# A state read followed by causal expert attention on one core: a new issue order, ScalarE's table asked for first, and 13 zero multiplications at the start left out

## The chip, the core and the metric

The kernel runs on one core of a Trainium2 chip. A core has TensorE (PE; its weight loads are listed as PEld), VectorE (DVE), ScalarE (ACT), GpSimd (POOL) and SyncE (SP), which issues every transfer here. The engines run side by side, each through its own list of instructions in order, and wait for each other by semaphores. The metric is the device time of one execution in microseconds (us).

## What is computed

There are two stages. For each of 8 batches and 8 heads, 512 rows of `x` and 32 rows of `state` (64 wide) attend to each other; the results, 544 rows of 512 columns in a batch, feed a causal attention with 4 experts, of which a gate takes the best two for each row:

```python
scores = scale * x @ state.T          # softmax over 32, then @ state -> xread
scores2 = scale * state @ x.T         # softmax over 512, then @ x    -> sread
x = concat([xread, sread])            # per batch: 544 rows, 512 columns
logits = x @ w_gate                   # two best of 4 experts, softmax of the two
for e in range(4):
    q, k, v = x @ wq[e], x @ wk[e], x @ wv[e]
    a = softmax(where(causal, -1e9, scale * q @ k.T))
    out += weight_of(e) * (a @ v @ wo[e])
```

Values that need more than fp16 are kept as two fp16 parts (high and low), and a product is the sum of three matmuls. The first batch is done in fp32 instead.

## The kernel before, in words

The kernel is a list of 2034 numbered steps. A step is one instruction of ACT, DVE, POOL or SP, or a group of matmuls; some steps have two or three ways, on different engines. Steps are first collected (`st.do`, `st.mm`, `st.dma`), batch by batch: `front` (loads `xn` and `sn`, transposes, the row softmax in `eb`, the attention `at` and the weights `gs` folded with the state, the gate, and `qm`, `kt`, `v`), `side` (the state's own rows), `main` (`probs`: scores, the exponential in `p`, its parts in `ph`, transposed by a transfer to `pt`; then `reads`: `pt` times `v`, scaled into `z`, split into `zh`, transposed by a transfer to `z`, multiplied by `wo_n`, and written out) and `tail` (the 32 last rows of two batches together).

Nothing in this text decides when a step runs. `run()` (line 346) goes through the table `ORDER` and issues the steps in that order. An entry such as `81.0.3` is step 81, way 0, and 3 zero multiplications ahead of it (line 360: 128x512 matmuls of the tile `zeros` into the PSUM bank that the step will write). The table `SLOTS` says which of several buffers each tile takes. Since each engine works through its list in order, the table decides what stands behind what on each engine, on SP's list of transfers too. Every step's instruction is recorded at line 362 (the call in `run()`), so rows of the profile are told apart by their tiles.

At the start, `zeros` is set by DVE (line 398). Step 0 is nine zero multiplications (`WARM=9`), which read no input. Steps 1 to 5 load the first batch's `sn` and `xn` (in four pieces of 256 KB, two for each half of the rows) and steps 7 and on the weights `wk`, `wq`, `wv` into three buffers `p`, each in a piece of three experts (384 KB) and one of one expert (128 KB). In `first` (line 662) step 8 transposes `sn` on TensorE, which ACT turns into the block-diagonal `tqf`; steps 69, 71, 131 and 133 transpose four tiles of `xn` (eight fp32 multiplications by `ident` each); steps 73 and 135 are the scores (`bank<-tqf,xT`); 83, 86 and 89 multiply the weights by the state (`bank<-p,tqf`), and 81 and 143 transpose the softmax's result (`bank<-ident,eb`).

Of batch 3 (counted from 0), step 977 is the transfer that transposes the probabilities of its last row block into `pt` (16 tiles of 128x128), and step 998 is the group of matmuls that reads them.

Of the kernel before, what the change touches and what calls it, by code (L numbers as in the profile page):

```python
# [9 lines left out]
F32 = mybir.dt.float32  # L10
# [19 lines left out]
2.0 3.0 44.0 42.0 32.0 61.0 52.0 33.0 56.0 55.0 51.0 0.0.2 186.0 184.0 1.0 8.0.11 69.0 185.0 71.0 5.0 4.0 131.0 30.0 31.0 11.0 13.0 38.0 50.0 64.0  # L30
65.0 62.0 6.0 66.0 7.0 67.0 133.0 9.0 70.0 10.0 188.0 72.1 187.0 189.0 190.0 132.0 191.0 73.0 134.0 198.0 201.0 74.0 75.0 76.0 135.0 218.0 86.0 136.0
77.0 68.0 63.0 137.0 88.0 87.0 78.1 79.0 222.0 12.0 83.0 324.0 322.0 207.0 85.0 138.0 80.1 323.0 89.0 139.0 91.1 22.0 47.0 54.0 40.0 28.0 43.0 46.0
58.0 48.0 18.0 140.0 203.0 141.0 142.1 81.0.3 195.0 204.0 82.0 325.0 90.0 223.1 336.0 119.0 143.0 333.0 144.0 206.0 337.0 205.0 326.0 96.0 172.0
210.0 330.0 120.1 334.0 92.0 149.0 145.0 331.0 219.0 224.0 45.0 53.0 41.0 14.0 327.0 173.0 35.0 93.0 97.0 239.0 100.0 211.0 328.0 24.0 200.1 26.0
15.0 29.0 202.1 16.0 19.0 199.1 60.0 338.0 192.0 84.1 101.0 104.0 102.0 105.0 103.0 98.0 150.0 99.0 146.0 153.0 154.0 157.0 209.1 106.0 107.0 231.1
155.0 158.0 121.0 226.1 147.0 335.0 159.0 122.0 332.0 94.0 329.0 108.0 156.0 160.0 109.1 174.0 161.0 162.1 175.0 240.0 197.1 148.0 110.0 180.0 176.0
123.0 163.0 111.0 164.0 165.0 112.0 220.1 95.0 166.0 113.0 167.0 168.0 114.0 170.0 171.0 151.0 115.0 181.0 118.0 117.0 152.0 124.0 221.0 228.0 193.1
208.1 232.0 196.1 182.0 339.0 177.0 125.0 340.0 347.0 346.0 127.0 588.0 37.0 233.0 348.0 128.0 229.0 194.1 230.0 591.0 225.1 241.0 183.0 169.0 126.0
116.0 341.1 342.0 178.0 179.0 243.0 592.0 593.0 442.0 244.0 129.0 130.0 242.0 370.0 343.0 358.0 246.0 359.0 245.0 360.0 252.0 253.0 349.1 227.0 594.0
344.1 350.0 351.0 254.0 255.0 345.0 247.1 373.0 249.0 20.0 34.0 443.0 361.1 248.0 352.1 362.0 439.0 265.0 266.0 256.0 250.2 257.0 258.0 353.0 259.0  # L40
590.0 215.0 444.0 589.0 375.0 374.0 363.0 267.0 268.0 445.1 251.0 262.1 364.1 376.0 354.0 234.0 365.0 595.0 1069.0 212.0 377.0 263.0 355.0 235.0
# [12 lines left out]
498.0 17.0 25.0 651.0 659.0 474.0 483.1 817.0 716.0 564.0 653.0 661.0 662.0 471.0 301.0 654.0 821.0 837.0 663.0 836.0 668.0 825.0 669.0 565.0 1079.0
818.0 717.0 822.1 664.0 665.0 1082.0 823.0 501.0 655.0 923.0 666.0 1080.0 1083.0 1070.0 484.0 316.0 718.0 670.0 719.0 503.0 485.0 683.0 667.0 720.0
671.0 824.0 317.0 819.1 504.0 486.0 826.0 499.0 562.0 1085.0 820.0 1084.0 698.0 515.0 1283.0 502.1 693.0 1086.0 838.0 672.0 566.0 567.0 673.0 924.0
36.0 21.0 505.0 674.0 675.0 487.0 920.0 506.0 684.0 488.0 516.0 827.1 676.0 686.0 689.0 828.0 1076.0 677.0 678.0 679.0 681.0 682.0 694.0 829.0 507.0
839.1 840.0 489.0 921.0 695.0 690.0 319.0 702.0 696.0 830.1 831.0 685.0 841.0 699.0 687.0 691.0 692.0 1081.0 318.0 1087.0 925.0 700.1 508.0 832.0
842.1 680.0 568.0 320.0 1077.0 703.0 517.1 520.0 697.0 848.0 853.0 843.0 688.0 704.0 1078.0 917.1 521.0 849.0 856.0 851.0 1284.0 854.0 833.0 569.0
705.0 701.0 522.0 512.0 509.0 857.0 852.0 850.0 721.0 722.0 730.0 731.0 922.0 706.0 1282.0 724.0 723.0 1281.0 1285.0 855.0 733.0 732.0 734.0 844.0  # L60
518.0 513.0 1088.0 834.0 835.0 523.1 510.0 845.0 1092.0 1095.0 570.0 725.1 726.0 727.0 743.0 728.0 511.0 1548.0 572.0 736.0 735.0 846.0 1093.1 729.0
737.1 519.0 738.0 524.0 571.0 573.0 574.0 918.0 1089.0 740.1 1094.0 1194.0 575.0 576.0 577.0 744.0 758.0 759.0 926.0 745.0 741.0 746.0 1096.0 1108.0
919.0 1189.1 1547.0 847.0 59.0 896.0 739.0 525.0 760.0 761.0 1107.0 927.0 1109.0 1090.1 747.1 1091.0 578.0 579.0 749.0 893.0 862.0 866.0 753.0 1191.1
1195.0 1196.0 1192.1 1292.0 742.1 762.0 1110.0 748.0 1295.0 897.0 763.0 764.0 750.1 751.0 1193.0 898.0 1296.0 1297.0 858.0 928.0 894.0 1111.0 859.0
929.0 863.0 768.1 867.0 1286.0 754.0 1097.0 1188.1 771.0 870.0 871.0 895.0 930.0 765.0 772.0 878.0 1098.1 755.1 1293.0 874.0 1099.0 879.0 880.0
1112.0 875.0 580.0 756.0 868.0 860.0 1100.0 876.0 869.0 1101.1 1113.1 864.0 526.0 1289.0 877.0 881.0 861.0 581.1 1102.0 304.0 903.0 529.0 882.0 766.0
# [1123 lines left out]
```

## Time and profile before

| | us |
|---|---|
| median of 3 runs | 292.83 |
| lowest and highest | 290.92, 296.96 |
| the profiled execution | 294.01 |
| its span in the profile | 292.2 |

In the span PE is busy 274.2 us, DVE 246.0, ACT 212.5 and POOL 198.2. The profile lists for every engine its instructions with start and length, and for each idle stretch what released the engine at its end. Three views are used: sums by stretch of time, the chain of work that ended last, and instructions in order of time. A matmul row with a count merges neighbours of one kind; fp32 multiplications count twice.

### The profile page before, as it was taken

To read this page: it belongs to the slowest core of one execution; us is meant where nothing else is said; L and a number is where in the kernel's file an instruction comes from. 1 tells how busy PE (TensorE), PEld (TensorE's weight loads), DVE (VectorE), ACT (ScalarE), POOL (GpSimd) and SP (SyncE) were. 2 spreads that over 40 slices of the span, in tenths; PEclk is the share of its full clock that TensorE was granted. 3 is DMA by queue.
4 is the path that set the end of the run, shared out by engine and by line. 5 is a ranking of instruction groups with operands and counts; after the bars stand their busy time and mean duration, and the time that the engine had idled before them with its cause. 6 is when DMAs were issued, how large, how long until landed. Compare 5 with 4: busy or idle time off the path is not lost.

```text
span 292.2 us, 9588 instructions
## 1 busy us (share of the span) xinstructions
PE 274.2 (94%) x3587; PEld 184.1 (63%) x3587; DVE 246.0 (84%) x787; ACT 212.5 (73%) x685; POOL 198.2 (68%) x268
## 2 busy tenths in 40 slices
PE   8989996989999989999999959999999999999994
PEld 3857753557557644877657637776566757666862
DVE  1489999999999988998999997989999987886540
ACT  3668897789889888987988885744977566366632
POOL 7144895688978988699985729989587646556200
PEclk9999999899999999999999999999999999999999
DMA  7946599899999999999999899998938966899673
GB/s 197 193 136 127 104 249 176 219 168 155 236 228 157 222 161 272 198 192 242 217 208 165 199 182 238 206 200 160 160 64 146 184 133 84 207 194 188 143 248 122
DMA packets 154574, 53.19 MB, mean 182 GB/s; under 512 B 140576, under 2 KB 150048, under 8 KB 154528
## 3 DMA queue, kind: packets, MB, share of 16 engines
q1 hardware_dynamic: 154528, 52.59, 94.6%
q8 instruction: 28, 0.46, 0.7%
q14 instruction: 18, 0.15, 0.1%
HBM read 11.02 MB, written 8.91 MB: 68 GB/s over the span
## 4 chain that ended last, share of the span: by engine, by line
PE 59%; DVE 26%; DMA 7%; issue 4%; ACT 2%; POOL 2%; DVEq 0%; ACTq 0%
PE bank L362 57%; DMA pt<-ph 5%; DVE xh L362 4%; DVE bank L362 3%; DVE gs L362 2%; DVE qf L362 2%; DVE sbm L362 2%; DMA qm<-qh 2%; DVE eb L362 2%; PE bank L360 2%; DVE m L362 2%; DVE mb L362 1%; DVE z L362 1%; DVE et L362 1%; POOL qh L362 1%
## 5 line engine op out<-in xcount | busy, mean ns | idle before, releaser
L362 PE MATMUL bank<-gs,at 128*128 128x260 f16 (+3 forms) x368 | 51.4, 285 | 1.8 <-ACT e L362 1.0
L362 PE MATMUL bank<-kt,qm 128*128 128x128 f16 (+13 forms) x368 | 48.0, 313 | 2.2 <-DMA qm<-qh 1.1
L362 PE MATMUL bank<-v,pt 128*128 128x192 f16 x480 | 44.0, 247 | 6.0 <-DMA pt<-ph 3.4
L362 PE MATMUL bank<-wo_n,z 128*128 128x512 f16 (+1 forms) x198 | 46.1, 373 | 1.0 <-DMA z<-zh 0.6
L362 PEld LDWEIGHTS <-pt 128*128 128x128 f16 x480 | 40.5, 98 | 9.6 <-DMA pt<-ph 6.6
L362 POOL TENSOR_TENSOR ph<-p,ph 128x1024 f16<-128x1024 f32 (+3 forms) x25 | 36.0, 1443 | 7.3 <-ACT ph L362 2.9
L362 PEld LDWEIGHTS <-at 128*128 128x128 f16 x336 | 32.7, 99 | 11.3 <-issue 3.3
L362 ACT ACTIVATE p<-bank,mx 128x128 f32<-128x128 f32 (+3 forms) x64 | 33.2, 525 | 3.5 <-DVE mx L362 2.6
L362 DVE CUSTOM_DVE_ANT_0 bank<-bank,causal 128x128 f32<-128x128 f32 (+3 forms) x64 | 30.6, 504 | 4.3 <-PE bank L362 4.0
L362 PEld LDWEIGHTS <-qm 128*128 128x128 f16 (+1 forms) x336 | 20.1, 96 | 18.0 <-issue 5.9
L362 PEld LDWEIGHTS <-z 128*128 128x128 f16 x198 | 18.6, 98 | 19.3 <-DMA z<-zh 1.2
L362 ACT ACTIVATE o<-bank 128x512 f32<-128x512 f32 (+1 forms) x35 | 20.3, 587 | 9.8 <-PE bank L362 9.2
L362 PE MATMUL bank<-at,gs 128*128 128x512 f16 (+1 forms) x100 | 24.7, 382 | 0.7 <-ACT at L362 0.7
L362 DVE SCALAR_TENSOR_TENSOR xh<-xn,xh 128x512 f16<-128x512 f32 x23 | 19.2, 854 | 5.2 <-ACT xh L362 5.2
L362 POOL TENSOR_SCALAR ph<-p 128x1024 f16<-128x1024 f32 (+3 forms) x12 | 11.1, 929 | 17.3 <-ACT p L362 11.8
L362 DVE TENSOR_TENSOR z<-bank,c 128x384 f32<-128x384 f32 x32 | 17.3, 548 | 5.1 <-PE bank L362 3.9
L362 POOL TENSOR_TENSOR zh<-z,zh 128x256 f16<-128x256 f32 x25 | 18.1, 728 | 4.6 <-ACT zh L362 3.3
L362 ACT ACTIVATE xh<-xn 128x512 f16<-128x512 f32 x32 | 19.4, 623 | 0.7 <-DMA xn<-in_x_dram 0.6
L362 POOL TENSOR_TENSOR qh<-qf,qh 128x384 f16<-128x384 f32 x18 | 16.3, 913 | 3.9 <-ACT qh L362 1.5
L362 POOL TENSOR_TENSOR a<-e,a 128x512 f16<-128x512 f32 x14 | 16.8, 1197 | 1.5 <-POOL mtail L362 0.9
L362 DVE SCALAR_TENSOR_TENSOR qf<-bank,m 128x384 f32<-128x384 f32 x32 | 17.0, 550 | 0.6
L362 ACT ACTIVATE gs<-bank 128x512 f16<-128x512 f32 (+3 forms) x32 | 14.5, 474 | 3.0 <-PE bank L362 2.9
(207 smaller groups left out, 649.4 us busy)
## 6 DMA issues: line engine op xcount, KB each, us to landing
out_dram<-o SPq DMA_DIRECT2D x33, 256.0 KB, 3.1
xn<-in_x_dram SPq DMA_DIRECT2D x14, 512.0 KB, 5.1
xn<-in_x_dram SPq DMA_DIRECT2D x4, 256.0 KB, 3.4
sn<-in_state_dram SPq DMA_DIRECT2D x8, 64.0 KB, 3.9
p<-in_moe_wo_dram SPq DMA_DIRECT2D x2, 256.0 KB, 4.5
xT<-xh SPq DMA_TRANSPOSE x28, 3.6
pt<-ph SPq DMA_TRANSPOSE x25, 4.8
p<-in_moe_wk_dram SPq DMA_DIRECT2D x1, 384.0 KB, 5.2
```

The lines of the kernel that those rows point to most:

```text
L360: self.nc.tensor.matmul(out=to[:, :], lhsT=self.zeros[:, :128], rhs=self.zeros, start=True, stop=True, skip_group_check=True)
L362: f(**{k: v.ap() if isinstance(v, View) else v for k, v in kw.items()})
```

## The change

Three things are changed. (1) Ahead of the constants, ScalarE gets one activation of one column with the function Exp, on `zeros`. Its table load is thereby the first thing on ScalarE's list. (2) `ORDER` and `SLOTS` are replaced. The 2 zero multiplications ahead of step 0 and the 11 ahead of step 8 are gone. Of the later ones, 3 stand ahead of step 119 in place of 3 ahead of 81, 5 ahead of step 388 in place of 4 ahead of 380, and the 2 ahead of step 1479 are gone. (3) With the new table, some steps take another way: of the small products for `c` (the softmax's denominators times the expert weights), 5 go from one DVE instruction to four ACT instructions, and splits of `z`, `qf`, `p` and `et` are dealt out anew among ACT, DVE and POOL. All 2034 steps are still there.

```diff
 ORDER = """
-2.0 3.0 44.0 42.0 32.0 61.0 52.0 33.0 56.0 55.0 51.0 0.0.2 186.0 184.0 1.0 8.0.11 69.0 185.0 71.0 5.0 4.0 131.0 30.0 31.0 11.0 13.0 38.0 50.0 64.0
+2.0 3.0 184.0 186.0 32.0 52.0 0.0 47.0 51.0 7.0 34.0 61.0 33.0 39.0 38.0 40.0 13.0 48.0 71.0 1.0 8.0 69.0 4.0 5.0 131.0 9.0 187.0 72.1 185.0 10.0
...
-    "ph": "1021201200120120201201201",
+    "ph": "0102011210210211010211201",
...
     st.zeros = zeros
+    table = const.tile([P, 1], F32, name="table")
+    nc.scalar.activation(out=table, in_=zeros[:, :1], func=AF.Exp)
     ident = const.tile([P, P], F32, name="ident")
```

The first place is the beginning on TensorE, from the last zero multiplication to the scores; tile numbers differ between the two programs (`xn_88` and `xn_90` are the same tile). Before:

```order
L360 MATMUL bank_82<-zeros 128x512
L362 MATMUL bank_82<-ident,sn_87 128x128
L362 MATMUL bank_81<-ident,xn_88 64x128 x8
L362 MATMUL bank_80<-ident,xn_88 64x128 x8
L362 MATMUL bank_84<-ident,xn_88 64x128 x8
L362 MATMUL bank_83<-ident,xn_88 64x128 x8
L362 MATMUL bank_81<-tqf_89,xT_101 128x2x32 x8
```

The row at the top is the last of 22 zero multiplications. Of the change, in the same place:

```order
L362 MATMUL bank_81<-zeros 128x512
L362 MATMUL bank_82<-ident,xn_90 64x128 x8
L362 MATMUL bank_85<-ident,sn_89 128x128
L362 MATMUL bank_83<-ident,xn_90 64x128 x8
L362 MATMUL bank_87<-ident,xn_90 64x128 x8
L362 MATMUL bank_88<-ident,xn_90 64x128 x8
L362 MATMUL bank_84<-tqf_91,xT_103 128x2x32 x8
```

Here the row at the top is the last of 9, and the first tile of `xn` has moved ahead of `sn`; behind the scores the multiplications of `wk` and `wq` (tiles `p_0`, `p_2`) now stand ahead of step 218. The second place is the beginning on ScalarE. Before:

```order
L362 ACT_TABLE_LOAD
L362 ACTIVATE xh_90<-xn_88 128x512 x2
L362 ACTIVATE tqf_89<-bank_82 64x4x32
L362 ACTIVATE xT_101<-bank_81 128x512
L362 ACTIVATE tqf_89<-bank_82 64x4x32
L362 ACTIVATE xh_92<-xn_88 128x512 x2
L362 ACTIVATE xT_101<-bank_84 128x512
L362 ACTIVATE xT_101<-bank_83 128x512
L362 ACTIVATE wn_77<-p_0_120 128x4x128 x2
L362 ACTIVATE eb_94<-eb_94 128x512
```

Of the change:

```order
L401 ACT_TABLE_LOAD
L401 ACTIVATE table<-zeros 128x1
L362 ACTIVATE xh_95<-xn_90 128x512 x2
L362 ACTIVATE tqf_91<-bank_85 64x4x32 x2
L362 ACTIVATE xh_92<-xn_90 128x512
L362 ACTIVATE xT_103<-bank_83 128x512
L362 ACTIVATE xh_92<-xn_90 128x512
L362 ACTIVATE wn_79<-p_0_122 128x4x128
L362 ACTIVATE xT_103<-bank_88 128x512
L362 ACTIVATE wn_79<-p_1_123 128x4x128
L362 ACTIVATE wn_79<-p_0_122 128x4x128
L362 ACTIVATE eb_96<-eb_96 128x512
```

One of the three copies of `xT` has gone to DVE, and the first exponential (`eb`) now has a split of `wv` (`p_1`) ahead of it too. The third place is SP's list around the transfer of step 977, here `pt_0_172` and `pt_0_174`. Before:

```order
L362 DMA_TRANSPOSE pt_0_164<-ph_153 128x12x128
L362 DMA_TRANSPOSE xT_101<-xh_92 128x8x128
L362 DMA xn_88<-in_x_dram 128x4x256
L362 DMA out_dram<-o_174 128x512
L362 DMA out_dram<-o_175 128x512
L362 DMA_TRANSPOSE pt_0_172<-ph_154 128x16x128
L362 DMA_TRANSPOSE z_169<-zh_171 128x8x128
L362 DMA xn_88<-in_x_dram 128x4x256
```

Of the change:

```order
L362 DMA_TRANSPOSE pt_0_166<-ph_156 128x12x128
L362 DMA_TRANSPOSE xT_103<-xh_92 128x8x128
L362 DMA out_dram<-o_178 128x512
L362 DMA_TRANSPOSE pt_0_174<-ph_155 128x16x128
L362 DMA xn_90<-in_x_dram 128x4x256
L362 DMA_TRANSPOSE z_170<-zh_172 128x8x128
L362 DMA xn_90<-in_x_dram 128x4x256
```

A load of `xn` (512 KB) and one of two writes (256 KB each) have gone from ahead of this transfer to behind it.

## Rows read from the trace of the kernel before

**Rows 1.** The page: busy us, share of the span and instructions of each engine.

```profile
PE 274.2 (94%) x3587; PEld 184.1 (63%) x3587; DVE 246.0 (84%) x787; ACT 212.5 (73%) x685; POOL 198.2 (68%) x268
```

**Rows 2.** Sums by stretch: start:end, length, busy of each engine, clock, transfers.

```profile
18.00:37.00 19.00, 17.58 (x145) 12.70 (x152) 17.88 (x62) 16.77 (x58) 11.39 (x15) 1.00 0.49 94
37.00:77.00 40.00, 35.50 (x574) 22.98 (x558) 39.32 (x119) 34.45 (x113) 31.72 (x38) 0.96 1.02 190
...
137.00:175.00 38.00, 35.05 (x507) 22.45 (x505) 35.22 (x124) 33.27 (x117) 25.74 (x30) 1.00 1.14 200
...
230.00:288.00 58.00, 58.00 (x658) 39.71 (x655) 40.02 (x138) 30.80 (x104) 23.86 (x29) 1.00 0.82 167
```

**Rows 3.** The chain that ended last, in order of time: start, us, what.

```profile
165.82 8.92 DMA pt<-ph
174.78 48.99 PE bank L362 x606
...
229.60 57.62 PE bank L362 x653
```

**Rows 4.** TensorE in order of time, 0 to 13: start, us, what, idle before.

```profile
2.00 4.05 PE L362 MATMUL bank<-zeros 128*128 128x512 bf16 x9
5.84 2.66 PE L360 MATMUL bank<-zeros 128*128 128x512 bf16 x11
8.34 0.27 PE L362 MATMUL bank<-ident,sn 128*128 128x128 f32 x1
8.54 3.71 PE L362 MATMUL bank<-ident,xn 128*64 128x128 f32 x64
12.18 0.99 PE L362 MATMUL bank<-tqf,xT 128*128 128x64 f32 x7
```

**Rows 5.** ScalarE in order of time, 0 to 16.

```profile
4.45 1.28 ACT L362 ACT_TABLE_LOAD   x1 [4.45 <-DMA xn<-in_x_dram]
5.74 1.15 ACT L362 ACTIVATE xh<-xn 128x512 f16<-128x512 f32 x2
8.71 0.27 ACT L362 ACTIVATE tqf<-bank 64x128 f32<-64x128 f32 x1 [1.82 <-PE bank L362]
...
15.67 0.63 ACT L362 ACTIVATE eb<-eb 128x512 f32<-128x512 f32 x1 [1.74 <-DVE eb L362]
```

**Rows 6.** SP's issues in order of time, 0 to 24.

```profile
2.58 1.14 SPq L362 DMA_DIRECT2D xn<-in_x_dram  x2
...
8.54 2.22 SPq L362 DMA_DIRECT2D p<-in_moe_wv_dram  x2
```

**Rows 7.** Transfers in flight at 3.7 to 4.3: count, KB, us from issue to landing.

```profile
xn<-in_x_dram SPq DMA_DIRECT2D x1, 256.0 KB, 4.0
```

**Rows 8.** The same at 8.5 to 9.1.

```profile
p<-in_moe_wv_dram SPq DMA_DIRECT2D x1, 384.0 KB, 5.0
```

**Rows 9.** TensorE in order of time, 12 to 24.

```profile
16.78 1.07 PE L362 MATMUL bank<-p,tqf 64*32 64x256 f32 x32
...
19.94 0.66 PE L362 MATMUL bank<-ident,eb 128*128 128x128 f32 x4 [0.44 <-DVE eb L362]
```

**Rows 10.** Sums by stretch around the fall of TensorE's clock.

```profile
43.40:50.40 7.00, 4.41 (x25) 2.46 (x26) 7.00 (x13) 6.19 (x16) 4.09 (x5) 1.00 1.07 176
50.40:53.90 3.50, 3.50 (x17) 1.99 (x15) 3.50 (x10) 1.65 (x5) 2.01 (x3) 0.51 0.76 143
```

**Rows 11.** SP in order of time, 155 to 184.

```profile
164.08 0.58 SPq L362 DMA_DIRECT2D xn<-in_x_dram  x1
...
165.82 4.83 SPq L362 DMA_TRANSPOSE pt<-ph  x1
```

**Rows 12.** TensorE in order of time, 161 to 182.

```profile
174.78 2.17 PE L362 MATMUL bank<-v,pt 128*128 128x192 f16 x24 [2.95 <-DMA pt<-ph]
```

**Rows 13.** Whom TensorE waited for: us in total, times, longest.

```profile
PE bank L362 <- DMA qm<-qh: 1.1, 1, 1.1
...
PE bank L362 <- DMA z<-zh: 0.6, 1, 0.6
```

More of the change, by code (lines that the diff above doesn't have):

```diff
@@ L29 @@
 ORDER = """
[90 rows of a table removed]
[90 rows of a table added]
 """
 SLOTS = {
-    "bank": ("032154267031452613153615264030231705321463753260413425310615720435606726314253170235106275210675460217125071562136107346"
-          "147206513742031563470214501376054321605423706352106752107564217352601024357610423715061240573165027316743132626270617423"
-          "07146750275134727651236540712451324160231675034572603175620643260415614356174356105617232403245104726103"),
-    "xh": "0231021302312013",
-    "p32": "01202102020102021021020102102120120201201",
-    "mb": "11000100",
-    "sbm": "10110100",
-    "m2": "01000010",
-    "bd": "0101010",
-    "kt": "012021020",
-    "s2": "01010101",
-    "lg": "0100110101011",
-    "gs1": "0010000101100",
-    "gt1": "0111010100101",
-    "a2": "0101010110101001",
-    "gs2": "0101001101010",
-    "gw": "0100100101001",
-    "m6": "10000101",
-    "qf": "10101010101010010101100101011001",
-    "a2t": "01110010",
-    "qm": "01110010",
-    "wgt": "01010101",
-    "mx": "21311032210321010330201320211301",
-    "sums": "01101001",
-    "ph": "1021201200120120201201201",
-    "xt_tail": "0010",
-    "c6": "0010101001010100",
-    "z32": "02101201201020202101210210201012",
-    "zh": "001110110100101",
-    "qh": "01101010101010",
-    "z": "001010110010101001",
-    "o": "2013122012301323010133202203121302",
-    "tw2": "0001",
-    "m4": "0001",
-    "tmt": "1101",
-    "twg": "0101",
@@ new lines @@
+    "xh": "3012031230210312",
+    "bank": ("014267350476321540517065102474703461701375402561732250376105237405612571430274653745063715067351237606105705731403576124"
+          "370165324076124764350132704216742065374602340512734051734063162713550273614250362514673104526365723153210345353261032617"
+          "03456216473025473047126530473623567035162735016045132740151476412753425734025734112034175372412536173425"),
+    "p32": "02110221110211020210210210210210211021002",
+    "mb": "00010101",
@@ new lines @@
+    "sbm": "10010010",
+    "m2": "00001101",
+    "bd": "0101010",
+    "kt": "021012012",
+    "gs1": "1001001010101",
+    "s2": "10101010",
+    "lg": "0110010010101",
+    "gt1": "0101111111111",
+    "a2": "1010011010100101",
+    "gs2": "1000011011100",
+    "gw": "0100010010101",
+    "m6": "10101001",
+    "qf": "01010101101010010101101010101010",
+    "a2t": "01010100",
+    "qm": "11110000",
+    "wgt": "01010010",
+    "mx": "02001332033201320132013210321003",
+    "sums": "10101010",
@@ L158 @@
+    "ph": "0102011210210211010211201",
+    "xt_tail": "1100",
+    "c6": "0000000101100110",
+    "z32": "01210121012012102101210102020210",
+    "zh": "101110010110101",
+    "z": "101010010110100100",
+    "qh": "10100101011001",
+    "o": "0120321210203221103021031302132102",
+    "tw2": "0110",
+    "m4": "0100",
+    "tmt": "1010",
+    "twg": "0100",
     "tmx": "0101",
     "tpt": "0111",
-    "tc4": "1011",
-    "tz": "10",
+    "tc4": "1010",
+    "tz": "01",
 }
```

178 rows, old and new, of the table ORDER are left out of this document.

## The prediction

> **What bounds the kernel now.** The page first: PE is busy 274.2 us of the span of 292.2, and no other engine more than DVE's 246.0 [rows 1]. That is an average over three stages, so the sums by stretch come next [rows 2]. From 18 to 77 DVE is full (17.88 of 19 us, then 39.32 of 40), while PE has holes. From 137 to 175 PE and DVE are about level (35.05 and 35.22 of 38); from 230 to 288 PE is closed, 58.00 of 58, and the others are slack. The chain of work that ended last says the same [rows 3]: its second half is 48.99 and 57.62 us of TensorE behind a transposing transfer of `pt` of 8.92. The reader is to see that a microsecond saved ahead of 18 or in a hole of PE behind 137 comes through to the end as long as DVE's work in between is no larger; work of ACT and POOL moved behind 230 costs nothing.
>
> The first 8 us are the other thing to see, on TensorE in order of time [rows 4]. The nine zero multiplications of step 0 start at 2.00 and the next eleven at 5.84, so one takes (5.84 - 2.00) / 9 = 0.427 us, which is 512 columns at 1.2 GHz; the eleven take 2.66, that is 0.24 us or less each, the 2.4 GHz level. So TensorE gained its full clock at about 6.0. The first real matmul, on `sn`, stands behind all 22 of them, at 8.34, while the first half of `xn` had landed at 4.45, where ACT stopped waiting for it [rows 5].
>
> **The change part by part.** *The zero multiplications at the start.* The first of all starts two before the nine, at 2.00 - 2 x 0.427 = 1.15. Nine from there end at 1.15 + 9 x 0.427 = 5.0, behind the landing at 4.45, so the first tile of `xn` can start at 5.0 in place of `sn` at 8.34: at most 3.3 us. Four tiles take 3.71 us at full clock, 0.93 each [rows 4]. The first lies mostly at half clock and takes some 1.5, to 6.5; `sn` takes 0.2, to 6.7; the second tile ends at 7.6. The second half of `xn` is issued by SP from 2.58 on, the later piece at about 3.2, and lands 4.0 us after it, at 7.2 [rows 6, 7]. The last two tiles end at 9.4, against 12.18 before. That is 2.8 us.
>
> *The table.* The load takes 1.28 us on ACT and stands behind the wait for `xn`, so `xh` starts at 5.74 [rows 5]. Asked for at the very beginning, it is done by about 2.5 and `xh` starts at 4.45. Taken alone this is worth nothing: ACT then waited 1.82 us for TensorE, until 8.71 [rows 5]. It pays since TensorE now comes 2.8 us earlier; otherwise `tqf` would be late by the 1.28.
> The Trainium skill (ScalarE: Activation LUTs, "What ACT_TABLE_LOAD costs") adds a drain of 1.38 us to such a load. By that rule the move would be worth 2.66 us on ACT, though still covered by TensorE; the row shows the first activation 0.01 us behind the load, so the sum goes by 1.28.
>
> *The new order up to the first softmax.* Scores (two groups, from 12.18 before) then run from 9.4 to about 13.2. The multiplications by weights began at 16.78 before [rows 9]; now those of `wk` and `wq` come right behind the scores, at about 13.2. Before, the large piece of `wv` landed at 8.54 + 5.0 = 13.5 [rows 6, 8]. In the new order on SP the three large pieces go first, so `wv`'s comes some 0.9 us earlier (128 KB of `wk` and 64 KB of `sn` fewer ahead of it, at some 200 KB/us [rows 2]), at 12.6, and the small one of `wk` at about 13.2. TensorE therefore hardly waits. ACT does: its first exponential was at 15.67 [rows 5] and now has a split of that `wv` and of that `wk` ahead of it, so it comes at 13.2 + 0.6 = 13.8, a gain of 1.9. The transposes of the softmax, at 19.94 before [rows 9], get between 1.9 and 2.8. I take 2.4 for the whole beginning, with 0 (all of it lost in ACT's list) and 3.3 as bounds.
>
> *DVE from 18 to 137.* I priced DVE's list row by row with the mean duration of each form, up to the same TensorE steps in both orders. To the first scores of batch 2 (104 us) it holds 85 us before and 86 now; to those of batch 3 (139 us) 116 and 115; in all 0.2 us more. The five small products that go from DVE to four ACT instructions each, and the re-dealt splits, put some 2.5 us on ACT, which is not the bound. So I take 0, with +-1.2 as bounds.
>
> *The hole at 174.78.* TensorE waited 2.95 us there for `pt` of batch 3's last block [rows 12]. SP issued that transfer at 165.82, behind a load of `xn` at 164.08 (512 KB) and two writes (256 KB each), and 8.92 us passed from there to the matmul [rows 3, 11]. Now only one write stands between `xT` and it. That takes about 1 us off the issue and 768 KB out of the way, at some 200 GB/s [rows 2] about 3.8 us. Against it, the scores that feed it end about 1.5 us of TensorE work later in the new order. Bounds 0 and 2.95; I take 2.0.
>
> *New holes.* An order dealt anew will have late transfers that I do not see. A single one is between 0 and the 2.95 us of the longest; the other single waits on a transposed tile were 1.1 and 0.6 [rows 13], so I charge 0.8, their mean. The later zero multiplications (3, 5 and none for 3, 4 and 2) stand in holes and count 0; without that cover one costs 0.24.
>
> **The sum.** 294.0 (the profiled execution: span 292.2 and 1.8 around it) - 2.4 - 2.0 + 0.8 = 290.4. That execution is 1.2 above the median of 292.83, so runs of the change should have a median of 289.2.
>
> **The rivals.** *The gain at the start is lost on the way, and the holes are only dealt anew.* For it: DVE is full for 59 us behind the start [rows 2], ACT's list is longer ahead of the first exponential, and TensorE has holes of 4.5 us between 37 and 77 alone [rows 2]. Against it: DVE's work to the same steps is equal within 1.2 us. Only 0.8 or less remains: 292.
>
> *All of it comes through, and more.* If the start gives 2.8, the hole at 174.78 all its 2.95, and the hole ahead of 50 also closes: there TensorE did 4.41 us of work in 7, and its clock was then at half (0.51) for 3.5 us [rows 10], which cost 3.5 / 2 = 1.75 us of work. 292.8 - 2.8 - 2.95 - 1.75 = 285.3.
>
> *Slower: the clock comes late.* At the start 4.9 us of dense zero multiplications stood ahead of the rise at 6.0 [rows 4]. Now there are 3.84, and then fp32 multiplications by `ident` on half the columns. If those do not bring the clock up, scores and weights run at 1.2 GHz too. Each us of TensorE work at half clock loses 0.5. The start's 2.4 is used up when the clock comes 4.8 us later than before, at 10.8; if it comes only behind the weights, near 18, the loss is 6 against 2.4, and with no gain elsewhere the time is 292.8 + 3.6 = 296.4. Against it: from 8.54 to 12.18 TensorE did nothing but such multiplications [rows 4] and ran at full clock.
> The Trainium skill (TensorE: Matmul & The Clock Gate, "What's actually happening") says that the throttled state is the default and activity releases it. By that rule fewer zero multiplications can only delay the rise; no run here has yet shown a start without them.
>
> *The change does nothing for the start.* If something other than the zero multiplications held `sn` until 8.34, TensorE would merely idle. That is unlikely: `xn` was there at 4.45. The time would be 292, as in the first rival.
>
> **How the numbers follow.** The forecast gets 0.45, its own range 287 to 291.5; the gain lost (with the change doing nothing) 0.27; all and more 0.18; the late clock 0.10. 2% of 292.83, about what a measurement of this kernel can tell from no change, is 5.9 us: faster means under 287.0, slower over 298.7. Faster: the 0.18 and a little of the forecast's lower end, 0.24. Slower: the worse half of the late clock, 0.05. Within: 0.71. The range for 8 in 10 runs from 284.8, which takes in the second rival, to 295.0, which leaves out only the upper end of the late clock.
>
> **What would show it.** TensorE in order of time: nine zero multiplications, then `xn` at 5.0, scores at about 9.4. ACT: the table load at about 0.8, `xh` at 4.45, the first `eb` at about 13.8. The transposes of `eb` at 17 to 18 in place of 19.94. DVE busy within 2 us of 246.0. No wait of 2.95 us for `pt` near 172. The prediction is wrong if `xn` starts at 5 and the first scores of batch 3 do not come some 2 us earlier than before (the DVE stage ate it), if the nine zero multiplications are followed by rows of doubled length past 8 us (the clock), or if TensorE waits for transfers more than before behind 137.

## The result and the profile after

Over 19 runs of each kernel the changed one has a median of 289.27 us (286.97 to 292.49), the one before 294.96 (290.92 to 297.46). The ratio is 0.9859, with a 95% interval of 0.9823 to 0.9895; it counts only runs within 1.5% of the fastest of their kernel (18 of 19 and 10 of 19), so it is not the quotient of the medians, which is 0.981. Of some 293 us that is 4.1 us, and 3.1 to 5.2 by the interval. The forecast was 289.2 us, or 3.6 us faster. The profiled execution of the changed kernel has a span of 288.7 us against 292.2.

The time is where it was forecast to be, but only in part did it come from where the forecast looked for it. The page and the sums by stretch first (columns as in [rows 1, 2]; the row PEclk is the granted TensorE clock in 40 equal slices, in tenths):

```profile
PE 270.6 (94%) x3571; PEld 182.2 (63%) x3573; DVE 242.5 (84%) x778; ACT 215.5 (75%) x707; POOL 197.9 (69%) x271
...
PEclk9979999999999999999999999999999999999999
```

```profile
18.00:37.00 19.00, 18.60 (x171) 13.53 (x154) 18.03 (x66) 16.10 (x57) 12.93 (x17) 0.98 0.75 139
37.00:77.00 40.00, 35.97 (x566) 22.74 (x565) 38.67 (x121) 36.68 (x122) 32.13 (x38) 1.00 1.07 196
137.00:175.00 38.00, 37.06 (x519) 23.29 (x517) 34.93 (x115) 32.12 (x110) 32.80 (x36) 1.00 1.14 202
230.00:288.00 58.00, 53.34 (x605) 35.88 (x602) 36.50 (x128) 30.55 (x106) 19.31 (x25) 1.00 0.73 152
```

TensorE still has 94% of the span. The 0.96 of its clock between 37 and 77 is gone (now 1.00), and the third slice, 14.4 to 21.7, is down to 0.7 instead. Between 137 and 175 TensorE works 37.06 us instead of 35.05: the hole at 174.78 has closed.

The start, on TensorE in order of time (start, us, what, idle before), in two pieces:

```profile
1.19 4.02 PE L362 MATMUL bank<-zeros 128*128 128x512 bf16 x9 [1.19 <-DVE zeros L398]
5.14 1.10 PE L362 MATMUL bank<-ident,xn 128*64 128x128 f32 x16
...
6.43 2.84 PE L362 MATMUL bank<-ident,xn 128*64 128x128 f32 x48
9.20 0.66 PE L362 MATMUL bank<-tqf,xT 128*128 128x64 f32 x4
```

```profile
14.86 1.53 PE L362 MATMUL bank<-p,tqf 64*32 64x256 f32 x32 [1.88 <-DMA p<-in_moe_wk_dram]
16.09 2.01 PE L362 MATMUL bank<-xT,tqf 64*32 64x512 f32 x16
17.79 1.16 PE L362 MATMUL bank<-p,tqf 64*32 64x256 f32 x16
...
19.09 0.60 PE L362 MATMUL bank<-ident,eb 128*128 128x128 f32 x4
```

Up to the scores everything is as forecast: `xn` at 5.14, the scores at 9.20 instead of 12.18. But then TensorE stands still for 1.88 us until the small piece of `wk` lands, and the 16 products `xT` by `tqf`, which took 1.09 us before, now take 2.01: the clock has fallen to 1.2 GHz, 0.58 on the mean from 14.8 to 18.9.

```profile
14.80:18.90 4.10, 4.04 (x80) 0.58 0.92 288
```

The transfers themselves were nearly idle in that wait (sums by stretch: start:end, length, clock, share of the transfer engines, GB/s; before it they moved over 200 GB/s):

```profile
12.00:13.00 1.00, 1.00 1.36 219
13.00:14.00 1.00, 1.00 0.41 32
14.00:15.00 1.00, 1.00 0.15 35
```

So the 3.0 us of the scores are 0.85 us at the `eb` transposes (19.09 instead of 19.94). On ScalarE in order of time the same wait stands ahead of the first exponential:

```profile
0.73 1.28 ACT L401 ACT_TABLE_LOAD   x1 [0.73 <-PEq L1178]
2.02 0.20 ACT L401 ACTIVATE table<-zeros 128x1 f32<-128x1 bf16 x1
4.59 1.15 ACT L362 ACTIVATE xh<-xn 128x512 f16<-128x512 f32 x2 [2.36 <-DMA xn<-in_x_dram]
...
14.84 0.63 ACT L362 ACTIVATE wn<-p 128x512 f16<-128x512 f32 x1 [1.28 <-DMA p<-in_moe_wk_dram]
15.37 0.61 ACT L362 ACTIVATE eb<-eb 128x512 f32<-128x512 f32 x1
```

To see where the rest came from, TensorE's steps were summed in both traces, each counted with the common length of its kind and without the zero multiplications. The lead at a time t of the kernel before is how much earlier the other kernel's TensorE had done as much. The kernels of the experiments below stand in the same table; "end" is 292.2 minus the span, and the last column is the ratio of device times to the kernel before.

| lead in us at | 9.4 | 20 | 45 | 54 | 116 | 126 | 170 | 180 | end | ratio, 95% interval |
|---|---|---|---|---|---|---|---|---|---|---|
| the change | 3.3 | 0.4 | 0.9 | 4.0 | 5.1 | 2.3 | 2.3 | 4.6 | 3.5 | 0.9859 (0.9823-0.9895) |
| the same, profiled again | 3.2 | 1.7 | 1.8 | 4.9 | 6.7 | 2.8 | 3.2 | 5.6 | 4.5 | 0.9880 (0.9819-0.9940) |
| start_old_order | 2.5 | 1.6 | 1.7 | 1.8 | 1.4 | 1.4 | 1.2 | 3.3 | 1.7 | 0.9971 (0.9924-1.0018) |
| order_only | 0.6 | 0.8 | 1.2 | 3.4 | 5.8 | 1.9 | 0.8 | 3.2 | 1.9 | 0.9878 (0.9804-0.9953) |
| no_table | 2.7 | 1.7 | 1.7 | 4.8 | 5.9 | 1.6 | -0.3 | 2.1 | 0.8 | 0.9926 (0.9883-0.9969) |
| scores_first | 3.3 | 1.6 | 2.0 | 5.1 | 6.1 | 2.0 | 0.6 | 2.9 | 1.8 | 0.9863 (0.9801-0.9926) |
| zeros_in_wait | 3.1 | 2.1 | 0.6 | 2.4 | 4.8 | 2.4 | 1.1 | 3.5 | 2.9 | 0.9897 (0.9818-0.9976) |
| pt_ahead_175 | 0.0 | 0.0 | 0.0 | 0.0 | 0.1 | 0.1 | -0.7 | 2.4 | 1.7 | 0.9914 (0.9876-0.9952) |
| pt_ahead_49 | -0.2 | -0.2 | -0.2 | 1.4 | -0.5 | -0.5 | -0.1 | -1.0 | -0.9 | 1.0046 (1.0003-1.0089) |
| loads_behind_116 | 3.5 | 2.2 | 1.9 | 5.0 | 6.5 | 5.0 | 4.7 | 7.1 | 5.9 | 0.9851 (0.9795-0.9907) |
| two_mended | 2.7 | 1.9 | 2.2 | 5.3 | 5.3 | 4.2 | 3.2 | 5.5 | 4.1 | 0.9837 (0.9782-0.9891) |

The first row has four large steps: 0.9 us from the start, 3.1 between 45 and 54, a loss of 2.8 between 116 and 126, and 2.3 back between 170 and 180. Two smaller ones cancel: 1.1 gained between 54 and 116, and 1.1 lost behind 180, where the new order has waits of 1.12 us for `pt` at 224.46 and 0.80 us for `tpt` at 278.14. Ratios of two kernels that differ by less than about 0.7% are not told apart here; the leads are one execution each, and the two profiles of the changed kernel differ by 1.0 us at the end.

### The profile page after: what moved, and what is told of

The parts are those of the page before. It is cut to its first block, busy times and chain, and to the rows that moved or that the text cites. A ratio compares the mean times of both kernels' runs of the same rounds, so it can differ in the third digit from the quotient of the medians.

```text
span 288.7 us, 9583 instructions
## 1 busy us (share of the span) xinstructions
PE 270.6 (94%) x3571; PEld 182.2 (63%) x3573; DVE 242.5 (84%) x778; ACT 215.5 (75%) x707; POOL 197.9 (69%) x271
## 4 chain that ended last, share of the span: by engine, by line
PE 60%; DVE 13%; DMA 12%; POOL 4%; ACT 4%; issue 3%; SPq 3%; DVEq 0%; ACTq 0%; POOLq 0%
PE bank L362 60%; DMA pt<-ph 6%; SPq L362 3%; DMA p<-in_moe_wk_dram 2%; DVE bank L362 2%; DMA qm<-qh 2%; DVE m L362 1%; DMA tpt<-ptl 1%; DVE z L362 1%; DVE qf L362 1%; DVE eb L362 1%; POOL z L362 1%; DVE xh L362 1%; DVE gs L362 1%; ACT p L362 1%
## 5 line engine op out<-in xcount | busy, mean ns | idle before, releaser
L362 PE MATMUL bank<-gs,at 128*128 128x260 f16 (+3 forms) x368 | 49.6, 282 | 0.4 <-ACT kt L362 0.2
L362 POOL TENSOR_TENSOR ph<-p,ph 128x256 f16<-128x256 f32 (+3 forms) x27 | 37.9, 1407 | 5.5 <-ACT bank L362 2.5
L362 DVE CUSTOM_DVE_ANT_0 bank<-bank,causal 128x256 f32<-128x256 f32 (+3 forms) x64 | 30.2, 506 | 6.2 <-PE bank L362 5.4
L362 ACT ACTIVATE p<-bank,mx 128x384 f32<-128x384 f32 (+3 forms) x64 | 33.3, 524 | 1.3 <-DVE mx L362 0.2
L362 PEld LDWEIGHTS <-z 128*128 128x128 f16 x198 | 18.6, 98 | 18.9 <-issue 1.4
L362 DVE SCALAR_TENSOR_TENSOR xh<-xn,xh 128x512 f16<-128x512 f32 x23 | 18.5, 815 | 5.0 <-ACT xh L362 4.9
L362 POOL TENSOR_TENSOR z<-z 128x128 f32<-128x128 f32 x24 | 12.1, 504 | 14.9 <-DVE z L362 13.7
L362 POOL TENSOR_SCALAR ph<-p 128x768 f16<-128x768 f32 (+3 forms) x13 | 10.5, 804 | 15.2 <-ACT p L362 8.6
L362 POOL TENSOR_TENSOR qh<-qf,qh 128x384 f16<-128x384 f32 x18 | 17.3, 970 | 4.9 <-ACT qh L362 3.9
L362 POOL TENSOR_TENSOR zh<-z,zh 128x256 f16<-128x256 f32 x22 | 15.6, 714 | 6.8 <-DVE zh L362 3.3
```

The costliest lines, as they stand in the source:

```text
L362: f(**{k: v.ap() if isinstance(v, View) else v for k, v in kw.items()})
```

## The experiments

**The two halves apart: the start alone, the order alone.** In the first, the old order with two entries changed and the table ahead; in the second, the new order with the zeros back and no table:

```diff
 # start_old_order (from the kernel before)
-... 51.0 0.0.2 186.0 184.0 1.0 8.0.11 69.0 ...
+... 51.0 0.0 186.0 184.0 1.0 8.0 69.0 ...
+    nc.scalar.activation(out=table, in_=zeros[:, :1], func=AF.Exp)
 # order_only (from the changed kernel)
-... 0.0 ... 71.0 ...
+... 0.0.2 ... 71.0.11 ...
-    nc.scalar.activation(out=table, in_=zeros[:, :1], func=AF.Exp)
```

> The kernel before with the two edits at the start alone: the 13 zero multiplications left out, the table asked for first, everything else in the old order. In the profile of the changed kernel TensorE's first scores came 3.0 us earlier (9.2 instead of 12.18), yet the `eb` transposes only 0.85 us (19.09 instead of 19.94), because the multiplication by the key weights waited for its load until 14.86 and the clock then fell. The old order loads those weights in one piece ahead of the others (landed by 9.6) and puts the scores' second half ahead of them. THEORY A (the start is worth 2.4 us to the end, as predicted): `eb` transposes at 17.3 to 18.0, and a device time 2 to 2.5 us under the kernel before, ratio 0.991 to 0.993. THEORY B (the start runs into the weights' landing and the rest is given back further on): `eb` transposes at 18.5 or later, ratio 0.996 to 1.000. The hole at 174.78 should stay, about 2.4 us earlier (A) or at its place (B).

> The changed kernel with the 13 zero multiplications put back (2 ahead of the first 9's end, 11 ahead of the first transposes) and without the early table: the new order alone. THEORY A (the sum as predicted: start 2.4, order 1.2): `eb` transposes 2 us or more later than the 19.09 of the changed kernel, device time 1.2 us under the kernel before, ratio 0.994 to 0.998. THEORY B (the weights' landing at 14.86 swallows the start in the new order, and the order brings the gain): the scores start at 12.2 again, TensorE comes to the key weights at about 16.0 without a wait and without a fall of the clock, `eb` transposes at 18.8 to 19.8, and the device time is within 0.8 us of the changed kernel's, ratio 0.985 to 0.989.

TensorE of the start alone, then of the order alone:

```profile
16.06 0.67 PE L362 MATMUL bank<-p,tqf 64*32 64x256 f32 x16 [1.08 <-DMA p<-in_moe_wq_dram]
...
18.20 0.60 PE L362 MATMUL bank<-ident,eb 128*128 128x128 f32 x4
```

```profile
12.09 3.79 PE L362 MATMUL bank<-tqf,xT 128*128 128x64 f32 x32
15.80 1.09 PE L362 MATMUL bank<-p,tqf 64*32 64x256 f32 x32
...
18.82 0.63 PE L362 MATMUL bank<-ident,eb 128*128 128x128 f32 x4
```

The start alone brings the `eb` transposes 1.7 us forward, between the two theories: even where `wk` is loaded in one piece, TensorE runs into a weight that has not landed, here the small piece of `wq` at 16.06. Most of it passes VectorE's busy stretches (1.4 at 116 and 126, 1.2 at 170). That 1.7 stand at the end again is chance: the hole at 174.78, whose transfer was not moved, was 2.0 us shorter in this execution, and 1.6 us were lost behind 180. The device time shows 0.3%, with 0 inside the interval, which just reaches Theory A's range too. The order alone, with all 22 zeros ahead, comes to the `eb` transposes at 18.82, earlier than the first profile of the full change, since it comes to the weights at 15.80 without a wait. It has 0.9878, nearly the whole gain and inside Theory B's range; the interval, up to 0.9953, does not shut out Theory A's 0.994 to 0.998, but the rows (no wait for the weights, `eb` at 18.82) came as Theory B has them.

**Does the wait for the weights cost more than its length?** Once the wait was filled with zeros, once with useful work, and once the table was left out:

```diff
 # zeros_in_wait: 8 zero multiplications ahead of the multiplication by wk
-... 135.0 86.0 136.0 ...
+... 135.0 86.0.8 136.0 ...
 # scores_first (each step keeps its PSUM bank)
-... 135.0 86.0 136.0 77.0 63.0 67.0 68.0 207.0 83.0 218.0 ...
+... 135.0 218.0 86.0 136.0 77.0 63.0 67.0 68.0 207.0 83.0 ...
 # no_table
-    nc.scalar.activation(out=table, in_=zeros[:, :1], func=AF.Exp)
```

> The changed kernel with 8 multiplications of zeros (1.7 us at the full clock) put where TensorE waits for the key weights, 12.98 to 14.86; they end before the weights land, so they delay nothing by themselves. THEORY B (the wait itself cost 1.9 us, and the half clock after it another 1.3): the granted clock stays full from 15 to 19 us, the steps from 14.86 to the `eb` transposes take 2.8 us instead of 4.2, `eb` at 17.7, device time up to 1.3 us under the changed kernel, ratio 0.981 to 0.984. RIVAL (the half clock there comes at another engine's expense only, or `eb` waits for ScalarE's exponentials): `eb` transposes earlier, but the end within 0.5 us, ratio 0.985 to 0.988.

> The changed kernel with one TensorE step moved: the 16 products `xT` by `tqf` (1.1 us at the full clock) run ahead of the multiplication by the key weights instead of two steps behind it, so that they stand where TensorE waited (12.98 to 14.86). THEORY B (the landing of the weights bounds the start): the wait shrinks from 1.9 to about 0.8 us, the `eb` transposes come at 16.9 to 17.5 if the clock stays full and 18 to 18.5 if it falls all the same; the device time falls by as much as reaches the end, 1 to 2 us, ratio 0.979 to 0.983. RIVAL (the stretch from 18 to 37 us hides it, since VectorE is busy nearly all of it): `eb` earlier but the end within 0.5 us of the changed kernel, ratio 0.985 to 0.988.

> The changed kernel without the early table: the load of ScalarE's table stands again in front of its first `xh`. ScalarE then begins `xh` at about 5.7 instead of 4.6 and copies `tqf` at about 7.8 instead of 6.6. THEORY B (the weights' landing near 14.8 bounds the start): the first scores slip from 9.2 to at most 10.4, TensorE still waits for the key weights (1.9 us less the slip), the `eb` transposes within 0.5 us of 19.09 and the device time within 0.5 us of the changed kernel's, ratio 0.984 to 0.988. THEORY A (the start is worth 2.4 us and the table is needed for half of it): 1.0 us or more slower than the changed kernel, ratio 0.989 or more.

With zeros in the wait the clock stayed full and the `eb` transposes came at 17.48. In that execution it was worth nothing: TensorE, then ScalarE of that kernel:

```profile
17.48 0.63 PE L362 MATMUL bank<-ident,eb 128*128 128x128 f32 x4
...
22.05 1.14 PE L362 MATMUL bank<-gs,at 128*128 128x260 f32 x4 [1.57 <-ACT gs L362]
```

```profile
20.82 0.63 ACT L362 ACTIVATE xh<-xn 128x512 f16<-128x512 f32 x1 [2.06 <-DMA xn<-in_x_dram]
21.36 0.64 ACT L362 ACTIVATE gs<-bank 128x256 f32<-128x256 f32 x2
```

ScalarE has the first split of batch 1's `xn` ahead of the `gs` that TensorE needs, and that `xn` landed only at 20.8. The lead falls from 2.1 at 20 to 0.6 at 45. Here the next landing set the time at 22, although the zeros ran on past the landing of `wk` (13.92 in this execution): the matmuls `bank<-gs,at` began at 22.05, against 21.95 in the first profile of the change, with the wait and the half clock. There `xn` was not what was waited for (its first split, at 20.35, follows its neighbour at once), and in the second profile, with a wait of 1.38 us, no fall and `xn` there at 19.64, they began at 20.86. So the wait and the fall did cost about 1 us in the first profile, and filling the wait pays only as far as `xn` lands early; the device time, 0.9897 (0.9818 to 0.9976), does not tell. With the scores put first the wait for `wk` was 0.50 us and the clock stayed full, but TensorE then waited 0.96 us at 17.02 for VectorE's `eb`, so the `eb` transposes came at 18.00, later than expected. The lead at 45 is 2.0, in which execution `xn` had landed by 19.40; the device time, 0.9863, is that of the change (the rival's range). Without the table the scores came at 9.79, TensorE waited 0.80 us for `wk`, and the `eb` transposes came at 17.85, as early as in the second profile of the full change (17.87). So the table moves nothing by the `eb` transposes, as Theory B has it; yet the device time is 0.9926, in Theory A's range and 0.7% above the change, with intervals that overlap. The profile places that loss between 116 and 170, far from the table; 1.13 us of it are a wait at 161.70 for ScalarE's `p`, which neither profile of the change has. Whether the table has a part in it is open.

**The hole at 174.78.** In the kernel before, only the transfer of step 977 was moved:

```diff
-... 1760.0 ... 782.0 ... 779.0 ... 977.0 ...
+... 977.0 1760.0 ... 782.0 ... 779.0 ...
```

> The kernel before with one transfer moved in SyncE's list: the transpose into `pt` for which TensorE waited 2.95 us at 174.78 goes ahead of the 512 KB load of `xn` and the two writes that stood in front of it (issue at 164.1 instead of 165.82). This is the step that was priced at 2.0 us in the forecast. AS FORECAST: the wait falls to 0 to 1 us and the device time by 2.0 us, ratio 0.991 to 0.995, with the lead kept from 175 to the end. RIVAL (VectorE or the tail takes it back): the wait falls, but the lead at 230 is under 1 us, ratio 0.997 to 1.000.

SyncE's issues in order of time, and the same matmuls on TensorE:

```profile
164.62 1.94 SPq L362 DMA_TRANSPOSE pt<-ph  x1
166.60 1.00 SPq L362 DMA_DIRECT2D xn<-in_x_dram  x1
167.66 1.12 SPq L362 DMA_DIRECT2D out_dram<-o  x2
```

```profile
172.40 2.16 PE L362 MATMUL bank<-v,pt 128*128 128x192 f16 x24
```

There is no wait left (2.95 us before, [rows 12]); the lead goes from -0.7 at 170 to 2.4 at 180 and 1.7 at the end, and the ratio of 0.9914 is 2.5 us (1.4 to 3.6 by the interval). Only the place of this transfer was changed, so the loads and writes ahead of it make the hole. How large it is depends on the execution: with the old SyncE list it was 2.95 us in the kernel before, 3.77 in `pt_ahead_49` (below) and 0.92 in `start_old_order`:

```profile
171.52 2.17 PE L362 MATMUL bank<-v,pt 128*128 128x192 f16 x24 [0.92 <-DMA pt<-ph]
```

The step between 170 and 180 in the table therefore measures the hole of the one execution that all are compared with, and `start_old_order` has such a step (2.1) without the move. The device times are what speaks for the term.

**The hole at 49.** The lead grows by 3.1 us between 45 and 54, from a hole that the forecast had left to a rival.

```diff
 # from the kernel before: the load of sn (step 1069) behind the transfer to pt (step 261)
-... 1069.0 ... 261.0 ...
+... 261.0 1069.0 ...
```

> The kernel before with one load moved in SyncE's list: the load of 64 KB of `sn` for batch 2 (issued at 40.65, taking SyncE 1.2 us, first used at 72.0) goes behind the first transpose into `pt` instead of two places ahead of it, as in the new order; the load of the output weights that stood between them is issued that much earlier. TensorE waited 2.59 us for that transpose at 49.19 and ran at half clock from 50.4 to 53.9 afterwards (1.75 us). In the changed kernel the wait is 0.93 us and the clock stays full; its lead grows from 0.9 us at 45 to 4.0 us at 54. THEORY F (these transfers in front make the wait, and the wait the fall of the clock): wait of 0.9 to 1.8 us, clock 1.00 from 50 to 54, a lead of 1.7 to 3.4 us at 54, device time 1.5 to 3 us under the kernel before, ratio 0.990 to 0.995. RIVAL G (the wait is made elsewhere, in the transposes' own landing time): wait within 0.5 us of 2.59, ratio 0.998 to 1.002. RIVAL H (the lead at 54 comes and is given back by 180, as VectorE is busy nearly all the time): ratio 0.996 to 1.000.

TensorE of that kernel and its sums by stretch, where the kernel before has [rows 10]:

```profile
49.42 1.66 PE L362 MATMUL bank<-v,pt 128*128 128x192 f16 x18 [2.60 <-DVE gs L362]
```

```profile
50.40:53.90 3.50, 2.82 (x24) 1.00 0.86 161
```

The wait is unchanged, so Theory F falls; the device time, 1.0046 (1.0003 to 1.0089), lies a little above the range of Rival G. The edit did not bring the transfer forward (issued at 43.73 instead of 43.49, right behind its `ph`), and in the new order the load of `sn` does not stand behind the transfer, as was expected, but farther ahead of it. The premise was misread too: what ends the wait is not the transfer but VectorE's `gs`, which empties the PSUM bank that the matmuls write into. This is the kernel before (TensorE, then VectorE), and then the changed kernel:

```profile
49.19 0.99 PE L362 MATMUL bank<-v,pt 128*128 128x192 f16 x10 [2.60 <-DVE gs L362]
```

```profile
46.56 1.64 DVE L362 SCALAR_TENSOR_TENSOR xh<-xn,xh 128x512 f16<-128x512 f32 x1
48.12 0.70 DVE L362 STREAM_TRANSPOSE et<-eb 128x512 f32<-128x512 f32 x1
48.75 0.38 DVE L362 SCALAR_TENSOR_TENSOR gs<-bank,gs 128x260 f16<-128x260 f32 x1
```

```profile
46.62 1.66 PE L362 MATMUL bank<-v,pt 128*128 128x192 f16 x18 [0.93 <-DVE gs L362]
```

```profile
45.13 1.10 DVE L362 SCALAR_TENSOR_TENSOR xh<-xn,xh 128x512 f16<-128x512 f32 x1
46.15 0.41 DVE L362 SCALAR_TENSOR_TENSOR gs<-bank,gs 128x260 f16<-128x260 f32 x1
```

In the old order the `gs` of that bank stands behind an `xh` and an `et` at 48.75; in the new one the bank (7 instead of 1) was last read by an earlier `gs`, at 46.15. Bank and VectorE's list together give 1.7 us. A run made for another question shows that this, and not the transfer, holds the old order: in `start_old_order` the first tile of `pt` was loaded at 45.60, 1.9 us before the matmuls, and the wait was 2.60 us all the same (weight load, VectorE, TensorE):

```profile
45.60 0.10 PEld L362 LDWEIGHTS <-pt 128*128 128x128 f16 x1 [1.29 <-DMA pt<-ph]
47.03 0.38 DVE L362 SCALAR_TENSOR_TENSOR gs<-bank,gs 128x260 f16<-128x260 f32 x1
47.47 1.28 PE L362 MATMUL bank<-v,pt 128*128 128x192 f16 x7 [2.60 <-DVE gs L362]
```

In the kernel before the transfer was late as well: its first tile was loaded at 48.59, so with a free bank 2.0 of the 2.60 us would have stayed in that execution. In the new order the `gs` leaves a wait of 0.93, and where the transfer landed later than that the wait was 1.77 (`order_only`) and 2.26 (`zeros_in_wait`). No run changes bank and list alone, so the 1.7 us are read from these rows. The run with the moved load shows one thing more: the clock happened to stay full behind the same 2.60 us wait. TensorE then led by 1.4 at 54 (it was 0.2 late at 45) and by 0.3 at 60: VectorE, busy through this stretch, took back 1.1 of these 1.6 us (TensorE waits 0.88 us at 54.16 for its next `gs`).

**The new hole at 116.** TensorE of the changed kernel, and SyncE ahead of it:

```profile
115.98 0.67 PE L362 MATMUL bank<-v,pt 128*128 128x192 f16 x6 [2.89 <-DMA pt<-ph]
```

```profile
106.67 0.65 SPq L362 DMA_DIRECT2D sn<-in_state_dram  x1
107.37 0.59 SPq L362 DMA_DIRECT2D xn<-in_x_dram  x1
108.01 0.61 SPq L362 DMA_DIRECT2D sn<-in_state_dram  x1
108.71 2.75 SPq L362 DMA_TRANSPOSE pt<-ph  x1
```

It is the pattern of 174.78 again: loads that nobody needs yet stand ahead of the transfer. A first attempt moved the transfer up, a second moved the loads away:

```diff
 # pt_ahead_116, and both_mended (with scores_first)
-... 1548.0 729.0 ... 738.0 ... 1282.0 1547.0 739.0 ...
+... 739.0 1548.0 729.0 ... 738.0 ... 1282.0 1547.0 ...
 # loads_behind_116, and two_mended (with scores_first)
-... 1281.0 ... 1548.0 ... 1282.0 1547.0 739.0 ...
+... 1281.0 1282.0 ... 739.0 1548.0 1547.0 ...
```

> The changed kernel with one transfer moved in SyncE's list: the transpose into `pt` that TensorE waits for at 115.98 (2.89 us; its `ph` was ready at 107.15, it was issued at 108.71 behind two loads of `sn` and one 512 KB load of `xn`, and landed 7.2 us later) goes ahead of those three loads, as it would have to in the old order at 174.78. In all runs so far TensorE's lead over the kernel before is 4.8 to 6.1 us at 116 and 1.9 to 2.4 us at 126. THEORY C (the loads ahead of it make the hole): issued at about 107.2, landed by 113, the wait under 0.7 us, the lead at 126 about 4.5 us, device time up to 2.5 us under the changed kernel, ratio 0.977 to 0.982. RIVAL D (VectorE takes the gain back between 137 and 175, where it was busy 35 of 38 us): the wait goes, the lead at 126 is 4 to 5 us, but at 170 it is no more than 3 and the end within 0.7 us of the changed kernel, ratio 0.984 to 0.988. RIVAL E (the wait moves to the `xh` made from the delayed `xn`): ScalarE waits for `xn` near 112 to 116.

> The changed kernel with the scores' second half ahead of the multiplication by the key weights (`eb` transposes at 18.0 instead of 19.09 when that was done alone, a lead of 6.1 us at 116) and the transpose for 115.98 ahead of the three loads. If the hole at 116 alone took back the gain of the first (lead 2.0 at 126 with it): lead 5 us or more at 126, device time 2.5 to 4 us under the changed kernel, ratio 0.973 to 0.978. If VectorE takes it back between 137 and 175: lead at 170 of 2 to 3 us, ratio 0.984 to 0.988.

Both were a mistake in the edit. The transfer also passed the steps 729 and 738, which write the low parts into `ph`, so one row block of batch 2 is computed with old low parts; and TensorE waits 5.0 and 5.4 us for GpSimd, which has those steps, near 115. Their ratios, 1.0075 (1.0031 to 1.0118) and 1.0079 (1.0037 to 1.0122), say nothing on the theories.

> The changed kernel as it is, profiled a second time. Leaving the table out left its profile 1.2 us earlier at the `eb` transposes and 2.7 us later at the end than the first profile of the changed kernel, and the hole near 115 was followed by half clock in it, in the order alone and in the scores put first, but not in the first profile of the changed kernel. If that is a matter of the execution: the second profile shows other waits in the start and a fall of the clock behind the hole at 115, a lead of 1.5 to 2.5 us at 126 whatever the lead at 116 was, and a ratio of 0.982 to 0.990. If it is the table's doing: `eb` transposes at 19.1 again, no fall at 115, and the lead at 170 over 2 us.

> The changed kernel with three loads moved away from the front of the transpose that TensorE waits for at 115.98: both loads of `sn` go behind it, the 512 KB load of `xn` goes to just behind its other half (issued at 100.55, while SyncE had to wait for `a` afterwards anyway). Each stays behind the steps that write its `ph`. THEORY C (the loads ahead of it make the hole): issued at 107.2 instead of 108.71 with nothing of them queued ahead of it, landed by 113, the wait under 0.7 us instead of 2.89, the lead at 126 about 4.5 us instead of 2.3, device time up to 2.5 us under the changed kernel, ratio 0.977 to 0.982. RIVAL D (VectorE takes it back between 137 and 175): the wait goes, the lead at 126 is 4 to 5 us, at 170 no more than 3, and the ratio 0.984 to 0.988. RIVAL G (the transpose itself takes that long whatever stands in front): it lands later than 114 and the wait stays over 1.5 us.

> The changed kernel with the scores' second half ahead of the multiplication by the key weights (alone: lead 6.1 us at 116, 2.0 at 126) and the three loads away from the front of the transpose for 115.98. THEORY C: the lead of 5 to 6 us passes 126, device time 2.5 to 4 us under the changed kernel, ratio 0.973 to 0.978. RIVAL D: lead at 170 of 2 to 3 us, ratio 0.982 to 0.987.

The second profile of the changed kernel has the hole too (2.31 us at 113.79), and behind it half clock, which the first had not:

```profile
114.00:118.00 4.00, 4.00 (x28) 0.57 1.16 295
```

Its `eb` transposes came at 17.87 instead of 19.09, so such differences in the start, and the fall here, come with the execution and need no table to explain them. Its lead is 6.7 at 116 and 2.8 at 126. Whatever the kernels with this SyncE list had at 116, from 4.8 to 6.7, they had 1.6 to 2.8 at 126. With the loads moved, SyncE and TensorE:

```profile
105.89 1.46 SPq L362 DMA_TRANSPOSE pt<-ph  x1
107.44 1.58 SPq L362 DMA_DIRECT2D sn<-in_state_dram  x2
```

```profile
111.48 0.66 PE L362 MATMUL bank<-v,pt 128*128 128x192 f16 x6
...
115.68 0.82 PE L362 MATMUL bank<-gs,at 128*128 128x260 f16 x6 [1.21 <-DVE kt L362]
```

The wait is gone, the clock stays full, and the lead is 5.0 at 126 and 4.7 at 170: Theory C for the hole. The span, 286.3, is 1.4 and 2.4 us below the two profiles of the change. The device time is not told apart: 0.9851, and 0.9837 with the scores first too, where the changed kernel in the same runs had 0.9880. Both ratios miss Theory C's ranges and lie in Rival D's, though the leads at 170, 4.7 and 3.2, are more than D allowed. So the cause of the hole is shown, but neither kernel is shown to beat the change.

## Why the prediction was right, point by point

- **The sum** came out at 289.2 against a median of 289.27, a drop of 1.2% against 1.4%. That the two times agree so closely is luck. It was made against a median of three runs, 292.83; with 19 runs that median is 294.96 and the profiled execution (294.01) lies below it, so the correction by 1.2 had nothing behind it.
- **The start, 2.4 us: too high.** Rows up to 9.4 came as worked out (table at 0.73, `xh` at 4.59, `xn` at 5.14, scores at 9.20), and the late clock did not happen: the first 16 transposes of `xn` took 1.10 us, the next 48 only 2.84. The step that failed is "TensorE therefore hardly waits". The small piece of `wk` was put at 13.2; it landed at about 14.8, 14.4 in the second profile. The piece of `wv` ahead of it came at 12.9, near the 12.6 worked out; the mistake was to take the rate for the landing. The trace marks 16 completions for a transfer, and it counts as landed with the last. For this piece 15 of them came between 12.37 and 12.95, as the rate says, and the last at 14.82 (13.44 and 14.35 in the second profile). TensorE waited 1.88 and 1.38 us for it, the first `eb` came at 15.37 instead of 13.8, and the start gave 0.9 and 1.8 us by 45. Had it been free of `wk`, the small piece of `wq` (landed at 15.3) and batch 1's `xn` (19.64 in the second profile, 20.82 in `zeros_in_wait`) were next. Device times say about 0.9 us for the start alone, with 0 inside the interval.
- **The table** was said to be worth nothing alone, which no run tests, and to spare `tqf` up to 1.28 us once TensorE comes earlier. Without it the first scores slipped by 0.59 us (9.79 for 9.20), and the wait for `wk` swallowed that; what it does to the device time stays open. The drain that the Trainium skill (ScalarE: Activation LUTs, "What ACT_TABLE_LOAD costs") adds to a load is not in the rows: the next activation is at 2.02, 0.01 us behind the load's end (0.73 + 1.28).
- **VectorE from 18 to 137, 0 us: right as a sum, wrong as a conclusion.** Its work is no smaller where it counts (18.03 and 38.67 us in the first two stretches, against 17.88 and 39.32; in all 242.5 for 246.0, outside the 2 us that I gave). But the order inside it decides when a PSUM bank comes free, and that took 1.7 us off the hole at 49. The rival "all comes through and more" had named this hole, and only as a possibility; it was the largest gain of the profile, 3.1 us with the clock.
- **The hole at 174.78, 2.0 us: right**, 2.5 by device time (1.4 to 3.6) when the transfer alone was moved. The upper bound, 2.95, was the hole of one execution; with the same SyncE list it was 0.92 and 3.77 in others.
- **New holes, 0.8 us: too low.** One alone, at 116, cost 2.8 us of lead, at the upper bound that I had given (2.95), and 3.9 in the second profile, where the clock fell behind it. The mean of two small waits was a poor price where the diff of SyncE's list could be read: a transfer with 640 KB of loads just ahead.
- In short, 2.4 + 2.0 - 0.8 = 3.6 was forecast; read from the first profile it was 0.9 + 3.1 - 2.8 + 2.3 = 3.5, with 1.1 more gained before 116 and lost again behind 180. The errors (the start 1.5 too high, the hole at 49 left out, the new hole 2.0 too low) cancelled, which is luck: of the three priced terms only the hole at 174.78 was right.

## What to carry to other kernels

Work removed at this kernel's start was worth only the way to the next landing: list the landing of every load that the following steps read, in the new order of issue, before pricing such a change, and leave room for a late share. A transfer that an engine waits for must not stand behind loads that are needed later; look for this in every order that is dealt anew, since it came back at another place. And a wait at a matmul can be for the PSUM bank that it writes, not for its inputs: the releaser in the row tells, and then the other engine's order is the thing to change. Look at what came second as well: behind the `gs` at 49 stood a transfer only 0.6 us earlier. A hole's size in one execution is not its price: the one at 174.78 was between 0.92 and 3.77 us.

## What was not expected of the hardware

The fall of TensorE's clock to 1.2 GHz did not follow from the length of the wait ahead of it. It came behind waits of 1.88 us (at 14.86), 2.60 (at 49.19 before) and 2.31 (at 113.79), but not behind 2.89 (at 115.98) or 2.60 (at 49.42), the last two with the same steps on either side as a wait that was followed by one. In two executions of one program it fell at different places. It also fell less often in the changed kernel: its mean granted clock was 0.996 or more in 14 of 25 executions, that of the kernel before in 10 of the 70 that have it on record. And what a fall costs depends on the next bound: without it 1.6 us were won near 50, of which VectorE took back 1.1 within 6 us, and behind 14.86 the wait and the fall together cost about 1 us (21.95 against 20.86 at `bank<-gs,at`), as the landing of `xn` came next.

A transfer lands with the last of its 16 completions. For the small piece of `wk` that was 1.9 us behind the other 15 (14.82 against 12.95) and 0.9 us in the second profile (14.35 against 13.44), with the transfer engines at 15% to 41% of their time while TensorE waited in the first; the landing worked out from bytes and rate alone was that much too early.
